# Writing the transposed keys and normalised rows contiguously, and reading them through permuted views

## The chip, the cores and the metric

The kernel runs on one core of a Trainium2 chip. The metric is the device time of one execution in microseconds (us). The engines are TensorE (PE, with its weight loads shown as PEld), VectorE (DVE), ScalarE (ACT), GpSimd (POOL) and SyncE (SP), which only issues DMAs here.

## What is computed

Three blocks follow one another on 8 x 576 rows of 512 numbers (all float32):

```python
# attention: 8 heads of 64, inside chunks of 64 rows
scores = scale * q_c @ k_c.T ;  attn = softmax(scores) ;  x = attn @ v_c
# first feed-forward block, w_ch1 512x2048, w_ch2 2048x512
xn = (x - mu) / sqrt(var + 1e-6) * g_ln
x1 = x + relu(xn @ w_ch1) @ w_ch2
# second block: a rank-32 mix along the 576 rows, then a feed-forward of the same size
u = x1 + (x1.T @ U @ V).T
out = u + relu(u @ w2_ch1) @ w2_ch2
```

## The kernel before, in words

The 4608 rows are 36 tiles of 128 rows. Attention and the first feed-forward work on twelve batches of three tiles. `g1` (L668) multiplies a batch with one of 16 slices of the first weight matrix: 12 matmuls of 384 columns into a PSUM tile `psh`, since each operand is split into a high and a low part and three of the four products are kept. ACT (L678) and DVE (L679) make the high and low parts of the result. `g2` (L682) multiplies these with the second matrix: 9 matmuls of 512 columns into `acc`. `finish` (L694) adds the sum to the residual. The loop at the end of `fused_kernel` writes the order of all this out by hand: one pair of `g1` and, two steps later, `g2` per step, with everything else hung on steps of that loop (`at`) or on thirds of a step (`at3`). An engine takes its instructions in exactly that order.

While one batch is multiplied, the attention and the normalisation of the tiles ahead are made beside it. Tiles 9 to 35 (27 tiles, the batches 3 to 11) go through these functions, in this order:

- `load_qk` (L329) brings q and k in by DMA, `st_A` (L377) turns both on DVE with a transpose that works on blocks of 32x32: L380 writes `qt`, L381 writes the key half of the tile `kt_pl`.
- `st_Bd` (L473) makes the scores with `quarters` (L368): 16 small float32 matmuls. `qt` is the stationary operand and `kt_pl` the moving one. The four quarters of the array are used side by side: two halves of the partitions (two heads) times two halves of the output (two chunks).
- `st_Cd`, `gather` and `st_T` (L504) turn the softmax weights, `st_D` multiplies them with v, `st_N` (L552) normalises: DVE at L563, then POOL at L564 times `g_ln`.
- `st_S` and `gather` send the normalised rows through HBM, and `st_E` calls `split` (L613): DVE turns them (L615) into a tile `wT`, ACT copies the high part into `act` (L617), POOL subtracts to get the low part (L618). `g1` of that batch reads both parts. `wT` and the normalised rows `xn` of the next tile share one buffer, so L563 of the next tile comes after L618.

Both transposes write their output through a view in which the 32 columns of a block lie four elements (16 bytes) apart: column number 4j + a, j counting 0 to 31 in the block and a the four blocks. So the reader finds the columns in natural order. Their inputs are read contiguously. The kernel's other block transposes are L504, L803 (reads 16 bytes apart, writes contiguously) and L965 (reads contiguously, writes 16 bytes apart). L661 is an ACT copy that reads 16 bytes apart.

In the same stretch the `pre_` functions (L183 to L266) prepare the weights of the second block on ACT and DVE and store them to HBM. After the last batch the second block runs, which the change does not touch.

Of the kernel before, what the change touches and what calls it, by code (L numbers as in the profile page):

```python
# [18 lines left out]
def fused_kernel(ctx, tc, q, k, v, g_ln, w1_a, w2_a, U, V, w1_b, w2_b, out):  # L19
    nc = tc.nc  # L20
# [20 lines left out]
    KT = DM // P  # L41
# [18 lines left out]
    def ps_tile(kind, shape):  # L60
        tags = banks[kind]
        turn[kind] += 1
        return psp.tile(shape, F32, tag=tags[turn[kind] % len(tags)], name="ps" + kind)

    def mm(o, l, r, start=True, stop=True, **kw):
        nc.tensor.matmul(o, lhsT=l, rhs=r, start=start, stop=stop, **kw)  # L66

    def f32(a):
        return a.bitcast(F32)
# [107 lines left out]
    pre = {}  # L177
# [149 lines left out]
    qk = {nm: qk6[:, 3 * m:3 * m + 3].rearrange("p t (a r i) -> p t a r i", a=4, r=4) for m, nm in enumerate(("q6", "k6"))}  # L327
# [15 lines left out]
    pl = {}  # L343
# [24 lines left out]
    def quarters(out, l, r):  # L368
        for pr in range(4):
            for h2 in range(2):  # L370
                pp = slice(64 * h2, 64 * h2 + 64)
                for c in range(2):
                    mm(out[h2][64 * c:64 * c + 64, ..., pr, :], l[pp, pr, 64 * c:64 * c + 64], r(pp, pr, c))
# [3 lines left out]
    def st_A(i):  # L377
        j, t = divmod(i, TPB)
        qt = t1.tile([P, 4, P], F32, tag="qt", name="qt")
        nc.vector.transpose(out=qt.rearrange("p r (j a) -> p a r j", a=4), in_=qk["q6"][:, t])  # L380
        nc.vector.transpose(out=pl["k"][:, 0].rearrange("p r (j a) -> p a r j", a=4), in_=qk["k6"][:, t])  # L381
        state["qt", i] = qt


# [88 lines left out]
    def st_Bd(i):  # L473
        qt = state.pop(("qt", i))
        sc = [ps_tile("m", [P, 2, 4, 32]) for _ in range(2)]
        quarters(sc, qt, lambda pp, pr, c: pl["k"][pp, 0, pr, 64 * c:64 * c + 64])
        m2 = st.tile([P, 2, 2, 2, 4], F32, tag="mx", name="mx")
        for h2 in range(2):
            nc.vector.tensor_reduce(out=m2[:, 0, h2].rearrange("p k r -> p (k r)"), in_=sc[h2].rearrange("p k r i -> p (k r) i"), axis=AX.X, op=ALU.max)
        nc.vector.tensor_tensor(out=m2[:, 1], in0=m2[:, 0, :, 0:1, :].to_broadcast([P, 2, 2, 4]), in1=m2[:, 0, :, 1:2, :].to_broadcast([P, 2, 2, 4]), op=ALU.max)  # L480
        e = t1.tile([P, DM], F32, tag="e", name="e")
        ev = e.rearrange("p (h g i) -> p h g i", h=2, i=32)
        for h2 in range(2):
            nc.vector.tensor_tensor(
                out=ev[:, h2], in0=sc[h2].rearrange("p k r i -> p (k r) i"),
                in1=m2[:, 1, h2].rearrange("p k (r o) -> p (k r) o", o=1).to_broadcast([P, 8, 32]), op=ALU.subtract,
            )
        nc.scalar.activation(out=e, in_=e, func=AF.Exp, scale=SCALE)
        state["e", i] = e
# [81 lines left out]
    def tiles_of(j):  # L571
        return [j * TPB + t for t in range(TPB)]

    def xt_tile(j, t):
        if t == 0:
            n = KT * P * len(tiles_of(j))
            o = (2 * n + 3 * BT) * (j % 2)
            xt[j] = tuple(act[:, o + m * n:o + (m + 1) * n].rearrange("p (k c) -> p k c", k=KT) for m in range(2))
        return (a[:, :, t * P:(t + 1) * P] for a in xt[j])
# [32 lines left out]

    def split(j, t, w, tag):  # L613
        x = t1.tile([P, KT, P], F32, tag=tag, name="wT")
        nc.vector.transpose(out=x.rearrange("p k (j a) -> p a k j", a=4), in_=w.rearrange("p a (k i) -> p a k i", k=KT))  # L615
        hi, lo = xt_tile(j, t)
        nc.scalar.copy(out=hi, in_=x)  # L617
        nc.gpsimd.tensor_tensor(out=lo, in0=x, in1=f32(hi), op=ALU.subtract)  # L618

# [3 lines left out]
    def st_E(i):  # L623
        split(i // TPB, i % TPB, state.pop(("w", i)), "xn")
# [497 lines left out]
    with tc.manual_schedule():  # L1122
# [23 lines left out]
        for n in range(2, NB):  # L1146
            g = NF * (n - 1)
            ends = []
            for t, i in enumerate(tiles_of(n)):
                if n == 2:  # L1150
                    s = (10, 15, 24)[t]
                    at(s - 6, load_qk_nat, i)
                    at(s, st_A_pe, i)
                    at(s + 1, st_B, i)
                    at(s + 2, st_C, i)
                    at(s + 3, st_D, i)
                    at(s + 3, load_v, i + 1)
                    if t == 0:
                        at(5, kv_tiles, i)
                        at(6, load_v, i)  # L1160
                    ends += [(pos[0, NF - 1] - 1 + t, st_N, i), (pos[0, NF - 1] + t, st_E_pe, i)]
                else:
                    s = g + {3: (2, 5, 8), 4: (-1, 2, 5), 5: (-2, 1, 5)}.get(n, (-3, 1, 5))[t]
                    at(s - (1 if n < 5 or t == 0 else 2), st_A, i)
                    at(s, st_Bd, i)
                    at(s + 1, st_Cd, i)
                    at(s + 2, gather, 2 * NT + i)
                    at(s + 3, st_T, i)
                    at(s + 5, st_D, i)
                    if i + 1 < NT:  # L1170
                        at(s + 5, load_v, i + 1)
                    s += 4 if n == 3 else 6
                    at(s + (n == 3), st_N, i)
                    at(s + 1, st_S, i)
                    at(s + 2, gather, i)
                    at(s + 3, st_E, i)
# [9 lines left out]
        for n in range(NB):  # L1186
# [6 lines left out]
            for t in range(TPB):  # L1193
                i = n * TPB + t
                r = i % 9
# [30 lines left out]
        free = [0, 0, 0]  # L1226
# [29 lines left out]
        x = PRE_G  # L1256
# [15 lines left out]
        for u in range(2 * NPR):  # L1272
# [2 lines left out]
            z = sums(u, y + 1)[1]  # L1275
            free[u % 2] = parts(u, z + g_pool, 1, 4)
            x += PRE_N[0]
        print("pre ends", free, file=__import__("sys").stderr)
        l2_first(at)

        load_qk_nat(0)
# [63 lines left out]
        for g in range(len(seq) + LAG):  # L1345
# [19 lines left out]
            j, f = seq[g - LAG] if LAG <= g < len(seq) + LAG else (0, 0)  # L1365
# [42 lines left out]
```

## Time and profile before

| | us |
|---|---|
| median of three runs (lowest to highest) | 1696.37 (1693.31 to 1698.58) |
| the profiled execution's own time | 1696.09 |
| its span, first to last instruction | 1694.2 |
| mean granted TensorE clock | 0.985 |

The span is what the trace shows; some 1.9 us of the time lie outside it. Matmul records overlap each other, so the busy time of PE says that something was in the array, not that it ran at its peak.

### The profile page before, as it was taken

How to read it: one execution, taken by the hardware profiler on the slowest of the kernel's cores; microseconds unless marked ns; L12 is line 12 of the kernel's file. 1: busy time of each engine (PE TensorE's matmuls, PEld its weight loads, DVE VectorE, ACT ScalarE, POOL GpSimd, SP SyncE). 2: the span in 40 equal slices, each digit the busy share in tenths (PEclk: the TensorE clock that was granted, in tenths of full speed). 3: DMA queues.
4: the chain of work that ended last, by engine and by line, in shares of the span. 5: the costliest groups of instructions: out<-in, count | busy, mean ns of one | idle time of the engine just before them, and what ended most of it. 6: DMA issues, size and time to landing. Idle time of an engine off the chain costs nothing.

```text
span 1694.2 us, 27810 instructions
## 1 busy us (share of the span) xinstructions
PE 1633.8 (96%) x9902; PEld 1423.1 (84%) x9902; DVE 1210.2 (71%) x2226; ACT 599.7 (35%) x1098; POOL 307.0 (18%) x291
## 2 busy tenths in 40 slices
PE   6899999999999999999999999999999999999997
PEld 5788878888788888888888899988887888888997
DVE  7887744577878787888874349739845983896496
ACT  5454411222232323323231134424443453334343
POOL 1000001111110211112021033043024303500421
PEclk8899999999999999999999999999999999999999
DMA  7353333546565556758553379888677887876885
GB/s 175 109 141 107 81 89 91 141 115 190 148 165 156 158 161 168 210 139 225 152 180 122 109 220 287 276 222 257 202 198 208 237 255 203 250 229 194 272 275 156
DMA packets 383948, 307.91 MB, mean 182 GB/s; under 512 B 192961, under 2 KB 280001, under 8 KB 383810
## 3 DMA queue, kind: packets, MB, share of 16 engines
q1 hardware_dynamic: 320802, 247.13, 52.3%
q10 hardware_dynamic: 63008, 59.00, 11.0%
q8 instruction: 80, 1.31, 0.3%
q14 instruction: 58, 0.48, 0.1%
HBM read 241.53 MB, written 64.49 MB: 181 GB/s over the span
## 4 chain that ended last, share of the span: by engine, by line
PE 62%; DMA 7%; DVE 4%; issue 1%; ACT 0%; SPq 0%; POOL 0%; ACTq 0%; DVEq 0%; POOLq 0%
PE ps L66 37%; PE acc L66 12%; PE psh L66 11%; DMA wr<-wd 3%; DMA zr<-zd 2%; PE psm L66 1%; DMA raw<-in_moe_w_ch 1%; DMA wd<-wsp 1%; PE zps L66 1%; PE pslow L66 1%; DMA wd<-wsq 0%; DVE zt L965 0%; DVE raw L228 0%; DMA out<-zt 0%; DVE act L679 0%
## 5 line engine op out<-in xcount | busy, mean ns | idle before, releaser
L66 PE MATMUL ps<-act,wr 128*128 128x512 f32 (+1 forms) x2100 | 445.7, 369 | 5.4 <-DMA wr<-wd 5.1
L66 PEld LDWEIGHTS ps<-act,wr 128*128 128x128 f32 x2100 | 382.8, 188 | 58.3 <-DMA wr<-wd 5.2
L66 PE MATMUL psh<-act,w0h 128*128 128x384 f32 x1536 | 398.9, 340 | 7.3 <-DVE act L679 2.7
L66 PE MATMUL acc<-w1h,act 128*128 128x512 f32 x1152 | 401.3, 402 | 1.5 <-DVE xbig L696 1.5
L66 PEld LDWEIGHTS psh<-act,w0h 128*128 128x128 f32 x1536 | 285.4, 191 | 27.1 <-DVE act L679 4.2
L66 PEld LDWEIGHTS acc<-w1h,act 128*128 128x128 f32 x1152 | 217.9, 189 | 58.8 <-issue 7.8
L66 PE MATMUL psh<-act,w0l 128*128 128x384 f32 x768 | 261.3, 340 | 0.9 <-DVE w0l L158 0.9
L679 DVE SCALAR_TENSOR_TENSOR act<-psh,act 128x384 fp32r<-128x384 f32 x192 | 106.7, 555 | 191.4 <-ACT act L678 190.9
L66 PE MATMUL acc<-w1l,act 128*128 128x512 f32 x576 | 228.8, 397 | 0.0
L678 ACT ACTIVATE act<-psh 128x384 fp32r<-128x384 f32 x192 | 93.8, 488 | 344.2 <-PE psh L66 279.5
L66 PEld LDWEIGHTS psh<-act,w0l 128*128 128x128 f32 x768 | 146.3, 190 | 1.2 <-DVE w0l L158 1.2
L66 PEld LDWEIGHTS acc<-w1l,act 128*128 128x128 f32 x576 | 109.0, 189 | 17.7
L618 POOL TENSOR_TENSOR act<-wT,act 128x512 fp32r<-128x512 f32 x27 | 34.9, 1293 | 307.2 <-ACT act L617 303.6
L544 POOL TENSOR_SCALAR rs<-mv 128x1 f32<-128x1 f32 x36 | 10.8, 301 | 402.7 <-DVE mv L542 394.4
L910 ACT ACTIVATE h<-h 128x512 f32<-128x512 f32 (+1 forms) x80 | 46.3, 588 | 102.8 <-DVE h L920 83.7
L916 DVE TENSOR_TENSOR h<-ps,h 128x512 f32<-128x512 f32 (+1 forms) x40 | 24.7, 632 | 69.7 <-PE ps L66 68.5
L197 ACT ACTIVATE raw<-raw 128x512 f32<-128x512 f32 x64 | 42.6, 674 | 55.0 <-DMA raw<-in_moe_w_ch 15.0
L654 POOL TENSOR_TENSOR zr<-zr 128x512 f32<-128x512 f32 x24 | 32.0, 1334 | 162.3 <-DMA zr<-zd 159.8
L903 POOL TENSOR_TENSOR h<-h,h 128x512 f32<-128x512 f32 (+1 forms) x40 | 51.8, 1316 | 36.2 <-DVE hr0l L890 15.6
L564 POOL TENSOR_TENSOR xn<-xn,gbc 128x512 f32<-128x512 f32 x27 | 38.6, 1428 | 50.2 <-DVE xn L563 50.2
L66 PE MATMUL ps<-hr0h,wr 128*128 128x512 f32 (+1 forms) x140 | 46.7, 373 | 0.3 <-issue 0.2
L66 PE MATMUL ps<-hr1h,wr 128*128 128x512 f32 (+1 forms) x140 | 46.0, 368 | 0.0
(218 smaller groups left out, 2558.3 us busy)
## 6 DMA issues: line engine op xcount, KB each, us to landing
wr<-wd SPq DMA_DIRECT2D x560, 256.0 KB
raw<-in_moe_w_ch SPq DMA_DIRECT2D x48, 512.0 KB
w<-sp ACTq DMA_DIRECT2D x54, 256.0 KB
wd<-wsp ACTq DMA_DIRECT2D x38, 256.0 KB
xw<-x1d SPq DMA_DIRECT2D x144, 64.0 KB
x1d<-xbig SPq DMA_DIRECT2D x34, 256.0 KB
v_pl<-in_v SPq DMA_DIRECT2D x132, 64.0 KB
out<-zt SPq DMA_DIRECT2D x132, 64.0 KB
```

Source lines behind the costliest of these rows:

```text
L66: nc.tensor.matmul(o, lhsT=l, rhs=r, start=start, stop=stop, **kw)
L197: nc.scalar.activation(out=w.bitcast(F32), in_=w.bitcast((F32, U32)[n]), func=AF.Copy, scale=2.0 ** (-112, -52)[n])
L544: nc.gpsimd.tensor_scalar(out=rs, in0=mv[:, 1:2], scalar1=1e-6, scalar2=None, op0=ALU.add)
L564: nc.gpsimd.tensor_tensor(out=xn, in0=xn, in1=gbc, op=ALU.mult)
L618: nc.gpsimd.tensor_tensor(out=lo, in0=x, in1=f32(hi), op=ALU.subtract)
L654: nc.gpsimd.tensor_tensor(out=zr[:, 0], in0=zr[:, 0], in1=zr[:, 1], op=ALU.add)
L678: nc.scalar.activation(out=hi, in_=ps, func=AF.Relu)
L679: nc.vector.scalar_tensor_tensor(out=lo, in0=ps, scalar=0.0, in1=f32(hi), op0=ALU.max, op1=ALU.subtract)
L903: nc.gpsimd.tensor_tensor(out=b11, in0=b12, in1=b11, op=ALU.subtract)
L910: relu = lambda a: nc.scalar.activation(out=a, in_=a, func=AF.Relu)
L916: vt(out=c12, in0=ps, in1=c12, op=ALU.add)
```

## The change

The two transposes write each block of 32 columns contiguously (column 32a + j in place of 4j + a). The readers get views that put the columns back in order: the score matmuls read `kt_pl` with a step of 32 elements inside groups of four, and so do ACT's copy and POOL's subtraction in `split`; what these two write is as before. A print at build time goes away. The transpose of q (L380) and that of the softmax weights (L504) stay.

```diff
 def st_A(i):
-    nc.vector.transpose(out=pl["k"][:, 0].rearrange("p r (j a) -> p a r j", a=4), in_=qk["k6"][:, t])
+    nc.vector.transpose(out=pl["k"][:, 0].rearrange("p r (a j) -> p a r j", a=4), in_=qk["k6"][:, t])
...
 def st_Bd(i):
-    quarters(sc, qt, lambda pp, pr, c: pl["k"][pp, 0, pr, 64 * c:64 * c + 64])
+    quarters(sc, qt, lambda pp, pr, c: pl["k"][pp, 0, pr].rearrange("p (a j) -> p j a", a=4)[:, 16 * c:16 * c + 16])
...
 def split(j, t, w, tag):
     x = t1.tile([P, KT, P], F32, tag=tag, name="wT")
-    nc.vector.transpose(out=x.rearrange("p k (j a) -> p a k j", a=4), in_=w.rearrange("p a (k i) -> p a k i", k=KT))
+    nc.vector.transpose(out=x.rearrange("p k (a j) -> p a k j", a=4), in_=w.rearrange("p a (k i) -> p a k i", k=KT))
     hi, lo = xt_tile(j, t)
+    x = x.rearrange("p k (a j) -> p k j a", a=4)
+    hi, lo = (a.rearrange("p k (j a) -> p k j a", a=4) for a in (hi, lo))
     nc.scalar.copy(out=hi, in_=x)
     nc.gpsimd.tensor_tensor(out=lo, in0=x, in1=f32(hi), op=ALU.subtract)
```

## Rows read from the trace of the kernel before

**Rows 1.** The page: busy time of PE and DVE, PE in 40 slices.
```profile
PE 1633.8 (96%) x9902; PEld 1423.1 (84%) x9902; DVE 1210.2 (71%) x2226; ACT 599.7 (35%) x1098; POOL 307.0 (18%) x291
...
PE   6899999999999999999999999999999999999997
```

**Rows 2.** Busy time by stage, 216 to 890: length, PE, PEld, DVE, ACT, POOL, clock.
```profile
216.00:890.00 674.00, 660.36 (x4798) 571.30 (x4797) 500.96 (x978) 188.48 (x358) 103.37 (x109) 1.00 0.56 155
```

**Rows 3.** Who PE waited for, 200 to 900: total, times, longest.
```profile
PE psm L66 <- DVE kt_pl L381: 10.7, 7, 3.6
...
PE psh L66 <- POOL act L618: 0.9, 1, 0.9
```

**Rows 4.** Groups of DVE: name, shapes, count, busy us, mean ns, idle before.
```profile
L615 DVE STREAM_TRANSPOSE wT<-w 128x512 f32<-128x512 f32 x27 | 29.6, 1098 | 8.7 <-DMA w<-sp 5.6 <-issue 1.9 <-DMA qk<-in_q 1.1
L380 DVE STREAM_TRANSPOSE qt<-qk 128x512 f32<-128x512 f32 x27 | 29.6, 1096 | 0.0
L381 DVE STREAM_TRANSPOSE kt_pl<-qk 128x512 f32<-128x512 f32 x27 | 29.1, 1078 | 0.0
...
L495 DVE TENSOR_REDUCE s<-e 128x16 f32<-128x512 f32 x27 | 17.7, 655 | 0.0
...
L106 DVE TENSOR_SCALAR qk<-qk 128x512 int32<-128x512 int32 x32 | 13.1, 409 | 0.0
...
L803 DVE STREAM_TRANSPOSE qk<-xw 128x512 f32<-128x512 f32 x10 | 11.0, 1096 | 0.0
...
L965 DVE STREAM_TRANSPOSE zt<-xbig 128x512 f32<-128x512 f32 x8 | 8.4, 1092 | 12.3 <-POOL xbig L949 12.3
```

**Rows 5.** Groups of ACT: a contiguous read and one 16 bytes apart.
```profile
L617 ACT CAST act<-wT 128x512 fp32r<-128x512 f32 x27 | 16.8, 621 | 61.6 <-DVE wT L615 61.6
...
L661 ACT CAST zs<-zr 128x512 fp32r<-128x512 f32 x8 | 8.8, 1106 | 13.9 <-POOL zr L654 13.9
```

**Rows 6.** Groups of POOL: the low part of the normalised rows.
```profile
L618 POOL TENSOR_TENSOR act<-wT,act 128x512 fp32r<-128x512 f32 x27 | 34.9, 1293 | 307.2 <-ACT act L617 303.6 <-DMA qk<-in_k 3.6
```

**Rows 7.** Timeline of PE at one score group: start, length, operation, records.
```profile
841.05 0.34 PE L66 MATMUL psh<-act,w0l 128*128 128x384 f32 x1
841.32 0.69 PE L66 MATMUL psm<-kt_pl,qt 64*64 64x64 f32 x32
841.94 0.50 PE L66 MATMUL acc<-w1h,act 128*128 128x512 f32 x1
```

**Rows 8.** The tile psm, 216 to 890: score matmuls, min/median/max ns.
```profile
L66 PE MATMUL psm<-kt_pl,qt x864: 218/218/312, 221.6 to 841.8; 64*64 64x64 f32 x173
```

**Rows 9.** Timeline of DVE before the longest wait for the keys.
```profile
424.62 0.56 DVE L679 SCALAR_TENSOR_TENSOR act<-psh,act 128x384 fp32r<-128x384 f32 x1 [0.85 <-ACT act L678]
...
429.12 1.06 DVE L380 STREAM_TRANSPOSE qt<-qk 128x512 f32<-128x512 f32 x1
430.04 1.04 DVE L381 STREAM_TRANSPOSE kt_pl<-qk 128x512 f32<-128x512 f32 x1
```

**Rows 10.** Timeline of DVE where two other such waits begin.
```profile
349.12 0.55 DVE L563 TENSOR_SCALAR xn<-xbig,mv,rs 128x512 f32<-128x512 f32 x1 [2.06 <-POOL act L618]
...
572.46 1.10 DVE L615 STREAM_TRANSPOSE wT<-w 128x512 f32<-128x512 f32 x1 [0.95 <-issue]
...
575.01 1.13 DVE L210 TENSOR_TENSOR raw<-raw,v_pl 128x512 f32<-128x512 f32 x1
```

**Rows 11.** Timeline of POOL: the subtractions at 574 and 666.
```profile
574.30 1.29 POOL L618 TENSOR_TENSOR act<-wT,act 128x512 fp32r<-128x512 f32 x1 [13.94 <-ACT act L617]
...
666.09 1.30 POOL L618 TENSOR_TENSOR act<-wT,act 128x512 fp32r<-128x512 f32 x1 [12.52 <-ACT act L617]
```

**Rows 12.** Timeline of PE: the first matmuls of batch 8.
```profile
668.02 0.51 PE L66 MATMUL psh<-act,w0h 128*128 128x384 f32 x2
```

More of the change, by code (lines that the diff above doesn't have):

```diff
@@ L1277, in fused_kernel @@
             x += PRE_N[0]
-        print("pre ends", free, file=__import__("sys").stderr)
         l2_first(at)
```

## The prediction

> **What bounds the kernel now.** I read the page first, then busy time by stage, then the waits. PE is busy for 96% of the span, and in every slice but the first two and the last at 90% or more [rows 1]. The changed operations run from 216 to 890 us. In these 674 us PE is busy for 660.4, DVE for 501.0, ACT for 188.5 and POOL for 103.4 [rows 2]. So PE sets the pace. Work taken off DVE can return at most what PE stood still, 674.0 - 660.4 = 13.6 us, while a matmul that takes longer is paid in full. The list of PE's waits says what of the 13.6 us the change can reach: 10.7 us in seven waits for the turned keys (L381), and 0.9 us in one wait for POOL's L618 [rows 3].
>
> The time is summed against the profiled execution's own 1696.09 us (span 1694.2 and 1.9 around it), which lies 0.3 us under the median, 1696.37.
>
> **The two transposes.** They take 1.078 us (keys) and 1.098 us (rows), 27 times each, as do all block transposes of 512 elements here; each of these has one side 16 bytes apart, the write in L380, L381, L615 and L965, the read in L803 [rows 4]. No row shows one with both sides contiguous. Ends: nothing is gained if turning 4-byte elements takes that long by itself; at best it runs like L106, 0.409 us. I take the nearest one-input pass over 512 floats, L495 with 0.655 us [rows 4], because on ACT the same 16-byte step accounts for a gap of that size: 1.106 us (L661) against 0.621 us (L617) [rows 5]. So L381 loses 0.42 us and L615 0.44 us. That is some 23 us less DVE work; what covers it is PE's own work, so only the waits count.
>
> **ACT's copy L617.** It now hops 128 bytes at every element. Ends: no cost if only the 16-byte step is slow, and L661's 1.106 us. I take the latter, the nearest row with scattered reads: +0.49 us [rows 5]. ACT has the room (188 of 674 us busy). Behind it in ACT's queue stands at most one L678, whose result `g2` needs two steps later; I cost that at nothing, and if the cover failed it would be 0.49 us at a place.
>
> **POOL's L618.** It takes 1.293 us [rows 6] and no row has POOL reading with a step. Ends: nothing, and a doubling, +1.29 us. I take ACT's surcharge per element, since it reads as many: +0.49 us. The end of L618 therefore moves by -0.44 + 0.49 + 0.49 = **+0.54 us**; between the ends, by -0.69 to +1.78 us.
>
> **What this does to the waits for the keys.** In each of the seven, L381 is the last thing to end. In the longest, DVE works without a pause from 424.62 to the end of L381 at 431.1, and nothing in that run gets shorter but L381 [rows 9]: 0.42 us back out of 3.6. Of the other six, five give 0.42 us too, and the smallest (0.25 us) vanishes: 6 x 0.42 + 0.25 = 2.8 us. Two of the seven runs begin at L618, though. At 349 us L563 starts only when L618 has let go of the shared buffer, after 2.06 us of idleness; at 575 us L210, right behind L615, is stretched to 1.13 us while L618 runs until 575.59 [rows 10, 11]. Both start 0.54 us later: +1.1 us. Sum for the keys: **-1.7 us** (ends: -5.8 and +3.6).
>
> **What it does at the start of a batch.** `g1` of the next batch needs the third tile's L618. Batch 3 waits for it already, so +0.54 us. Batch 8 has the smallest margin of the others: L618 ends at 667.39, the first matmul is at 668.02, 0.63 us [rows 11, 12]; the other seven, read the same way, have 1.26 to 2.36 us. These cover 0.54 us. Sum: **+0.5 us** (ends: -0.7 and, with the margins used up, +5.2).
>
> **The score matmuls.** This is the term that decides. They are the only changed work on PE itself: 27 groups of 16 float32 matmuls, two records each, 864 in all [rows 8]. One group holds PE from 841.32 to 841.94, 0.62 us [rows 7]. With four quarters of the array at work side by side, 32 records are eight rounds of 0.078 us, and a round streams 64 key columns. Before, four neighbours lay in 16 bytes; after, each column is 128 bytes from the last. No row shows PE reading with a step. Lower end: nothing, if PE fetches far enough ahead. A middle value: ACT pays (1106 - 621) / 512 = 0.947 ns more per scattered element [rows 5]; for 64 columns and eight rounds 0.485 us a group, 27 x 0.485 = 13.1 us. Upper end: the two halves of the output read the same 64 partitions, so the two key streams of a pair may have to take turns, 128 elements a round, 26.2 us. I take **+13.1 us**: in the rows a scattered step costs alike on every port that shows one, DVE's read, DVE's write and ACT's read [rows 4, 5], and float32 on PE leaves little slack, since a round of 0.078 us has 1.2 ns per column, less than the 1106 / 512 = 2.2 ns that ACT needs for one. The pause comes inside PE's own stream, with nothing to hide it; only what other engines owe PE gets easier by it.
>
> [...]
>
> **Sum.** 1696.09 - 1.7 + 0.5 + 13.1 = 1708.0 us, 0.7% slower.
>
> **The rivals.** *PE does not notice.* The reads are 64 columns long and could be fetched ahead while weights load; a 384-column record takes 0.34 us [rows 7], 0.9 ns a column, so PE's port delivers more than ACT's does. Against: the rates above. Then -1.7 + 0.5 remain: 1694.9 us, no change.
>
> *The two halves take turns.* For it: both streams of a pair lie in the same partitions, and today's score groups draw on four streams at once. Against: contiguous streams show no sign of it. 1696.09 - 1.2 + 26.2 = 1721.1 us. [...]
>
> *Faster: DVE catches up.* If PE reads the keys for nothing and 23 us less DVE work let DVE reach L381 ahead of PE, all seven waits and the one for L618 close: 1696.09 - 10.7 - 0.9 = 1684.5 us. It decides once L381 ends earlier by as much as the wait is long, up to 3.6 us. Against it: the run at 424 us starts from a wait for PE's own results and holds one shortened operation of 0.42 us.
>
> *The transposes do not get faster.* All show 1.08 to 1.10 us, whichever side has the step, so the time could be the transposer's. Then L618 ends 0.98 us later: two key waits +2.0, batch 3 +1.0, batch 8 +0.35; with the readers' price 1696.09 + 3.3 + 13.1 = 1712.5 us, without PE's part 1699.4.
>
> **How the numbers follow.** The forecast has 0.46, the unaffected PE 0.25, the two halves in turn 0.15, DVE catching up 0.06, transposes as slow as before 0.08 (0.06 with PE's price, 0.02 without). A measurement of this kernel tells about 0.3%, 5 us, from no change. Slower: 0.46 + 0.15 + 0.06, less 0.02 for a price on PE too small to be seen, 0.65. Same: 0.25 + 0.02 + 0.02 = 0.29. Faster: 0.06. The range starts at 1693, two microseconds under the case of an unaffected PE for the ends of the small terms, and goes to 1723, the same above the two halves in turn; it leaves out the faster case and the far ends.
>
> **What would show it.** Right: L381 and L615 near 0.66 us with L380 and L504 at 1.1; L617 near 1.1 and L618 near 1.8 us; the score group near 1.1 us from its first record to the next `acc` matmul; waits for L381 about 9 us in sum. Wrong: a score group still at 0.62 us (then no change), or at 1.6 us (then 1721), transposes still at 1.08 us, or no wait for L381 left.

## The result and the profile after

The changed kernel takes 1704.25 us, the median of seven runs (1701.03 to 1711.68); the kernel before, run beside it, 1696.37. The ratio is 1.0056 with a 95% interval of 1.0035 to 1.0076: slower, by some 9.5 us (5.9 to 12.9). The profiled execution took 1703.15 us, its span is 1701.3. From L617 on the line numbers are two higher: ACT's copy is now L619, POOL's subtraction L620.

The groups of the changed operations first (the columns as in [rows 4]), from the views of DVE, ACT and POOL:

```profile
L504 DVE STREAM_TRANSPOSE kt_pl<-w 128x512 f32<-128x512 f32 x27 | 29.7, 1101 | 10.6 <-DMA w<-sp 10.6
L380 DVE STREAM_TRANSPOSE qt<-qk 128x512 f32<-128x512 f32 x27 | 29.6, 1096 | 0.0
L615 DVE STREAM_TRANSPOSE wT<-w 128x512 f32<-128x512 f32 x27 | 19.1, 707 | 5.9 <-DMA w<-sp 3.1 <-issue 1.4 <-DMA qk<-in_q 1.3
L381 DVE STREAM_TRANSPOSE kt_pl<-qk 128x512 f32<-128x512 f32 x27 | 18.3, 679 | 0.0
...
L619 ACT CAST act<-wT 128x512 fp32r<-128x512 f32 x27 | 31.0, 1146 | 47.4 <-DVE wT L615 47.4
...
L620 POOL TENSOR_TENSOR act<-wT,act 128x512 fp32r<-128x512 f32 x27 | 43.1, 1597 | 309.1 <-ACT act L619 305.6 <-DMA qk<-in_k 3.6
```

DVE's two transposes fall from 1078 and 1098 ns to 679 and 707, while L380 and L504, not touched, stay at 1.1 us [rows 4]. The readers pay: ACT's copy goes from 621 to 1146 ns [rows 5], POOL's subtraction from 1293 to 1597 [rows 6].

What PE pays, in its timeline at one score group and in the list of the tile `psm` (min/median/max ns of 864 records):

```profile
849.43 0.34 PE L66 MATMUL psh<-act,w0l 128*128 128x384 f32 x1
849.70 1.11 PE L66 MATMUL psm<-kt_pl,qt 64*64 64x64 f32 x32
850.74 0.51 PE L66 MATMUL acc<-w1h,act 128*128 128x512 f32 x1
...
L66 PE MATMUL psm<-kt_pl,qt x864: 273/287/305, 222.0 to 850.5; 64*64 64x64 f32 x173
```

The group now holds PE from 849.70 to 850.74, 1.04 us where it was 0.62 [rows 7], and the record in the middle is 287 ns long where it was 218 [rows 8]. Over the 27 groups the mean rises from 0.630 to 1.044 us: 27 x 0.414 = 11.2 us.

Against that stand the waits (total, times, longest):

```profile
DVE xn L563 <- POOL act L620: 8.6, 3, 2.9
...
PE psm L66 <- DVE kt_pl L381: 8.1, 6, 2.6
```

PE waits 8.1 us for the keys in place of 10.7 [rows 3]; in the same list `xn`, which shares its buffer with `wT`, waits 8.6 us for POOL in place of 6.2. The last row that the prediction did not reckon with is the granted clock. Two stretches of the view of busy time by stage, and the whole stage (columns as in [rows 2]):

```profile
289.30:292.70 3.40, 3.40 (x10) 2.47 (x8) 2.28 (x6) 1.74 (x2) 1.14 (x1) 0.50 0.21 34
436.10:439.40 3.30, 3.30 (x10) 2.65 (x9) 3.20 (x9) 0.48 (x1) 0.00 (x0) 0.50 0.12 24
216.00:890.00 674.00, 664.49 (x4757) 574.12 (x4757) 485.40 (x964) 199.97 (x350) 108.06 (x107) 0.99 0.56 153
```

In both short stretches PE is never idle and has a clock of 0.50; both come soon after one of the long waits for the keys. In the first one a pair of 512-column matmuls takes 1.05 us (at 289.55), in the kernel before, at a clock of 1.00, 0.62 (at 288.21). By an estimate from the granted clock alone a stretch of 3.4 us at 0.50 does what takes 1.7 us at 1.00, so it costs up to 1.7 us. The changed kernel has two such stretches in this stage. The kernel before has one, after its longest wait:

```profile
431.60:435.00 3.40, 3.40 (x30) 2.70 (x23) 3.26 (x9) 0.00 (x0) 0.00 (x0) 0.51 0.39 106
```

The account for the stage: groups +11.2, waits for the keys -2.6, the wait at the start of batch 3 -0.7 (0.9 to 0.2), the wait for the residual (`xbig`) at its start -0.3 (1.57 to 1.25), two small waits that are gone (`g1` for L679 and for L617) -0.4, one more stretch at half clock +1.7, together +8.9 us. The first matmul of batch 11 came at 887.63 us before and comes here, in PE's timeline, at

```profile
896.43 0.51 PE L66 MATMUL psh<-act,w0h 128*128 128x384 f32 x2
```

which is 8.8 us later, as the account has it. These are the rows of one execution of each kernel. What follows, the last batch and the second block, takes 804.8 us to the end of the span (806.6 before), a scatter of that size being usual there: 801.7 to 808.7 in the experiments, none of which touches it.

### The profile page after: what moved, and what is told of

Read it like the earlier page. It is cut to its first block, busy times and chain, and to the rows that moved or that the text cites. A ratio compares the mean times of both kernels' runs of the same rounds, so it can differ in the third digit from the quotient of the medians.

```text
span 1701.3 us, 27810 instructions
## 1 busy us (share of the span) xinstructions
PE 1644.2 (97%) x9902; PEld 1432.1 (84%) x9902; DVE 1200.7 (71%) x2226; ACT 614.6 (36%) x1098; POOL 315.3 (19%) x291
## 2 busy tenths in 40 slices
DMA packets 383948, 307.91 MB, mean 181 GB/s; under 512 B 192961, under 2 KB 280001, under 8 KB 383810
## 4 chain that ended last, share of the span: by engine, by line
PE 64%; DMA 5%; DVE 4%; issue 1%; SPq 0%; POOL 0%; ACT 0%; DVEq 0%; POOLq 0%
PE ps L66 35%; PE acc L66 14%; PE psh L66 13%; DMA zr<-zd 2%; PE psm L66 2%; DMA xw<-x1d 1%; PE zps L66 1%; PE pslow L66 0%; DMA x1d<-xbig 0%; DVE zt L967 0%; DMA wr<-wd 0%; DMA raw<-in_moe_w_ch 0%; DMA wd<-wsq 0%; DVE xbig L827 0%; POOL zr L656 0%
## 5 line engine op out<-in xcount | busy, mean ns | idle before, releaser
L681 DVE SCALAR_TENSOR_TENSOR act<-psh,act 128x384 fp32r<-128x384 f32 x192 | 106.6, 555 | 213.8 <-ACT act L680 213.1
L620 POOL TENSOR_TENSOR act<-wT,act 128x512 fp32r<-128x512 f32 x27 | 43.1, 1597 | 309.1 <-ACT act L619 305.6
L544 POOL TENSOR_SCALAR rs<-mv 128x1 f32<-128x1 f32 x36 | 10.8, 301 | 404.3 <-DVE mv L542 396.0
L619 ACT CAST act<-wT 128x512 fp32r<-128x512 f32 x27 | 31.0, 1146 | 47.4 <-DVE wT L615 47.4
```

Of the source, the lines that this page charges most:

```text
L544: nc.gpsimd.tensor_scalar(out=rs, in0=mv[:, 1:2], scalar1=1e-6, scalar2=None, op0=ALU.add)
L681: nc.vector.scalar_tensor_tensor(out=lo, in0=ps, scalar=0.0, in1=f32(hi), op0=ALU.max, op1=ALU.subtract)
```

## The experiments

Each ratio is that of an experiment to the kernel before, run on the same chip.

### The two halves apart

`e1_rows_only` leaves the keys as they were:

```diff
-        nc.vector.transpose(out=x.rearrange("p k (j a) -> p a k j", a=4), ...)
+        nc.vector.transpose(out=x.rearrange("p k (a j) -> p a k j", a=4), ...)
+        x = x.rearrange("p k (a j) -> p k j a", a=4)
+        hi, lo = (a.rearrange("p k (j a) -> p k j a", a=4) for a in (hi, lo))
```

> Only the rows' half of the change: L615 writes contiguously, ACT's copy and POOL's subtraction read through the view; the keys are as before. Theory (the loss is PE's read of the keys): score groups stay at 0.62 us to the next matmul, L615 0.71, the ACT copy 1.15, the POOL subtraction 1.6 us; no change, 1695 to 1698 us (+0.0 to +0.1%). Rival (the loss comes from the rows, whose low part is ready later at batch starts and behind which DVE work queues): 5 us or more over before, 1701 or more.

Measured: 1.0020 (1.0002 to 1.0038), 3.4 us. L615 takes 706 ns, ACT's copy 1144, POOL's subtraction 1594; the score group stays at 0.64 us. The waits for the keys are 11.7 us in nine, more than before, and three stretches (286.6, 358.2 and 433.3 on) run at half clock. So the time falls between the two cases: the theory had at most 0.1%, the rival 5 us or more.

`e2_keys_only` is the other half:

```diff
-        nc.vector.transpose(out=pl["k"][:, 0].rearrange("p r (j a) -> p a r j", a=4), ...)
+        nc.vector.transpose(out=pl["k"][:, 0].rearrange("p r (a j) -> p a r j", a=4), ...)
...
-        quarters(sc, qt, lambda pp, pr, c: pl["k"][pp, 0, pr, 64 * c:64 * c + 64])
+        quarters(sc, qt, lambda pp, pr, c: pl["k"][pp, 0, pr].rearrange("p (a j) -> p j a", a=4)[:, 16 * c:16 * c + 16])
```

> Only the keys' half of the change: L381 writes contiguously and PE reads through the view; the rows are as before. Theory: score groups 1.04 us, 27 x 0.42 = 11.3 us dearer, the waits for L381 2.6 to 2.8 us less in sum: 1704 to 1706 us (+0.5%). Rival (the loss comes from the rows): no change or faster, 1693 to 1697 us.

Measured: 1.0040 (1.0022 to 1.0057), 6.8 us. L381 takes 678 ns, the group 1.044 us, the waits for the keys 5.7 us in five; they fall by 5.0 us, not by the 2.6 to 2.8 that were expected. Groups and waits make 11.2 - 5.0 = 6.2 us. The two halves add up to 0.60% where the whole change costs 0.56%: as far as intervals of 0.2% to either side tell, they don't act on each other.

### The key half taken apart

`e3_read_only` has the new view for PE and the old transpose:

```diff
-        quarters(sc, qt, lambda pp, pr, c: pl["k"][pp, 0, pr, 64 * c:64 * c + 64])
+        quarters(sc, qt, lambda pp, pr, c: pl["k"][pp, 0, pr].rearrange("p (a j) -> p j a", a=4)[:, 16 * c:16 * c + 16])
```

`e4_turn_only` has the new transpose and the old view:

```diff
-        nc.vector.transpose(out=pl["k"][:, 0].rearrange("p r (j a) -> p a r j", a=4), ...)
+        nc.vector.transpose(out=pl["k"][:, 0].rearrange("p r (a j) -> p a r j", a=4), ...)
```

> The kernel before with one edit: PE reads the keys through the view with a step of 32 elements, while L381 writes as before, so the scores have their keys in another order than v has. Theory: the price on PE alone, 27 x 0.42 = 11.3 us, and the waits for L381 stay near 10.7: 1706 to 1709 us (+0.65%). Rival (the step is not what costs, the tile written in runs of 32 is): score groups 0.62 us, 1695 to 1698 us.

> The kernel before with one edit: L381 writes contiguously, PE reads the tile contiguously, so the scores have their keys in another order than v has. Theory: what the cheaper transpose gives back without PE's price: L381 0.68 us, score groups 0.62 us, waits for L381 near 8.0 in place of 10.7: 1693 to 1695 us (-0.15%). Rival (DVE catches up with 11 us less work): waits for L381 under 3 us, 1688 us or less.

Measured: e3 1.0072 (1.0049 to 1.0096), e4 0.9988 (0.9970 to 1.0007). In e3 the group takes 1.044 us with a transpose of 1081 ns, so the pause is PE's reading and nothing else:

```profile
L381 DVE STREAM_TRANSPOSE kt_pl<-qk 128x512 f32<-128x512 f32 x27 | 29.2, 1081 | 0.0
...
L66 PE MATMUL psm<-kt_pl,qt x864: 273/287/304, 221.3 to 846.7; 64*64 64x64 f32 x173
```

(Its waits for the keys fall to 7.2 us where 10.7 were expected, perhaps because a slower PE leaves DVE time; the profiled execution was the shortest of nine, 1696.19 against a median of 1703.65, so its rows don't show all of the 0.72%.) In e4 the group takes 0.625 us, and of the waits this is left:

```profile
PE psm L66 <- DVE kt_pl L381: 5.6, 5, 1.7
```

The faster transpose alone saves 5.1 us of waits in the profile, where 2.8 were forecast for it (three executions below, with the same work on DVE, save 3.0 to 3.9), and the comparison can't tell the time from no change. The waits don't close: DVE does not catch up with PE.

### Which pattern costs PE its pause

Three single profiled runs, all with the new transpose of the keys, each with another view for PE (the added lines in the order `e5_runs16`, `e6_pairs`, `e7_step16`). They took 1691.97, 1695.32 and 1704.35 us, where nine runs of the kernel before have a median of 1690.35; one run each is too few to compare times, so the groups are read:

```diff
-  pl["k"][pp, 0, pr, 64 * c:64 * c + 64]
+  pl["k"][pp, 0, pr].rearrange("p (a j) -> p a j", a=4)[:, :, 16 * c:16 * c + 16]
+  pl["k"][pp, 0, pr].rearrange("p (a j w) -> p j a w", a=4, w=2)[:, 8 * c:8 * c + 8]
+  pl["k"][pp, 0, pr, 64 * c:64 * c + 64].rearrange("p (j a) -> p a j", a=4)
```

> The keys' half of the change, but PE reads each chunk in four runs of 16 adjacent columns, so the keys of the scores stand in another order than in v. If the price is for elements whose neighbour lies elsewhere, 4 breaks in 64 columns cost next to nothing: a score group takes 0.62 to 0.66 us to the next matmul. Rival (a view of two dimensions costs by itself): 1.04 us.

> As before it, but PE reads pairs of adjacent columns, 128 bytes from pair to pair (keys in another order than in v). If a port runs at full speed once it finds two elements in the same 16 bytes, a score group stays at 0.62 to 0.70 us. Rival (every break costs the same): half the breaks, half the price, 0.62 + 0.21 = 0.83 us.

> As before it, but PE reads with a step of 16 bytes (four elements) in runs of 16 columns (keys in another order than in v). If what counts is that no two elements that follow each other share 16 bytes, a score group takes 1.04 us as with the step of 128 bytes. Rival (the distance counts): between 0.62 and 0.95 us.

The records of the score matmuls in the list of the tile `psm`, runs of 16 columns, then pairs, then single columns 16 bytes apart:

```profile
L66 PE MATMUL psm<-kt_pl,qt x864: 218/218/313, 222.1 to 838.4; 64*64 64x64 f32 x173
```

```profile
L66 PE MATMUL psm<-kt_pl,qt x864: 213/216/288, 220.9 to 839.0; 64*64 64x64 f32 x173
```

```profile
L66 PE MATMUL psm<-kt_pl,qt x864: 273/292/308, 220.8 to 850.2; 64*64 64x64 f32 x173
```

The groups take 0.635, 0.628 and 1.071 us. Pairs of neighbours with 128 bytes from pair to pair take no longer than the contiguous read (0.628 us, 0.630 before). Single columns cost about as much with a step of 16 bytes as with one of 128. So it is neither the length of the hop nor the number of hops as such. In these runs the price came with single columns 16 or 128 bytes apart (1.071 and 1.044 us) and not with pairs of neighbours (0.628 us); e11_pairs_both below, with a step of 8 bytes, adds that two columns of 16 bytes that are not neighbours are enough (0.639 us). No row shows why that is so.

### Two ways out that keep the contiguous transpose

With PE reading runs of 16 columns the scores come out in another key order. `e8_runs16_v` loads v in that order too, so the softmax weights meet the right rows:

```diff
+                    vs = v[b, h2::2, s * CH:(s + 1) * CH, :].rearrange("h (j a) d -> a j h d", a=4)
+                    for a in range(4):
+                        p0 = 64 * h2 + 16 * a
+                        nc.sync.dma_start(out=pl["v"][p0:p0 + 16, 0, :, c, :], in_=vs[a])
```

> A version without PE's price: keys turned with contiguous writes, PE reads four runs of 16 columns a chunk, and v is loaded in the same order of keys, with four DMAs of 16 partitions in place of one of 64. Theory: L381 0.68 us, score groups 0.62 to 0.66 us, waits for L381 near 5.6 us: -0.1 to -0.3% against before. Rival (the 12 more DMA issues a tile, some 8 us of SP's time each tile, make k or v late): waits for v or for k's load on PE or DVE, no gain or slower.

Measured: 1.0445 (1.0421 to 1.0468), with groups of 0.659 us. Its waits, and its DMA issues of v:

```profile
ACT raw L197 <- DMA raw<-in_moe_w_ch: 49.8, 11, 9.4
...
PE psm L66 <- DVE kt_pl L387: 21.1, 8, 8.0
...
PE psm L66 <- DMA v_pl<-in_v: 8.8, 3, 6.2
```

```profile
v_pl<-in_v SPq DMA_DIRECT2D x432, 16.0 KB
v_pl<-in_v SPq DMA_DIRECT2D x24, 64.0 KB
```

432 loads of 16 partitions have taken the place of 108 of 64, and data that come by DMA are late: ACT waits 49.8 us for the weights (15.0 before), PE 8.8 us for v itself (0.2 before). The clock falls with it: its mean over the five runs is 0.970, against 0.988 in the nine of the kernel before, by an estimate from these means some 33 us of the 75 that were lost (0.030 x 1764 less 0.012 x 1688). The price came back in DMA, eight times the cost of the whole change. Which part of it is issuing on SP and which the smaller transfers was not separated.

`e9_psum_scatter` puts the hop on PE's output instead: the keys are read in four runs of 16 per matmul, and each result column is written to its place in PSUM, 16 bytes from the last:

```diff
+                kv_ = pl["k"][pp, 0, pr].rearrange("p (a c k j) -> p c a k j", a=4, c=2, k=2)
+                    o = sc[h2][64 * c:64 * c + 64, :, pr, :].rearrange("p k (j a) -> p a k j", a=4)
+                    mm(o, qt[pp, pr, 64 * c:64 * c + 64], kv_[:, c])
```

> A version that computes the reference: keys turned with contiguous writes (rows as before), PE reads each chunk in four runs of 16 adjacent columns, and puts the keys back in order where it writes: into PSUM, with a step of four elements. Theory (only the read from SBUF costs): score groups 0.62 to 0.66 us, waits for L381 near 5.6 us, -0.1 to -0.3% against before. Rival (a scattered write to PSUM costs as the scattered read does): score groups near 1.0 us, +0.4%.

The records of the score matmuls:

```profile
L66 PE MATMUL psm<-kt_pl,qt x864: 218/218/267, 221.0 to 837.3; 64*64 64x64 f32 x173
```

Measured: 0.9994 (0.9981 to 1.0007), groups of 0.625 us, L381 at 677 ns, waits for the keys 7.0 us. A step of 16 bytes, which costs 0.44 us a group on the read (e7_step16), costs nothing on the write to PSUM (0.625 us, as in e4_turn_only with a contiguous write). The time can't be told from no change. The waits of single executions also scatter: e4_turn_only, e5_runs16, e6_pairs and this kernel have the same work on DVE and groups of the same length, and show 5.6, 6.8, 7.7 and 7.0 us of waits for the keys.

### What the rows half pays

`e10_rows_read` has the new views for ACT and POOL and the old transpose: the readers' price without the transposer's gain.

```diff
+        x = x.rearrange("p k (a j) -> p k j a", a=4)
+        hi, lo = (a.rearrange("p k (j a) -> p k j a", a=4) for a in (hi, lo))
```

> The kernel before with one edit: ACT's copy and POOL's subtraction of the rows read through the view, while L615 writes as before, so the rows come out in another order. This has the readers' surcharge (0.52 and 0.30 us) without the cheaper transpose. Theory (the rows' half costs through the later end of POOL's subtraction, by 0.83 us here against 0.44 in the rows' half alone): +0.2 to +0.3%, waits of L563 and of PE for the subtraction longer than with the rows' half alone. Rival (the +0.2% of the rows' half is scatter between runs): within 0.1% of before, waits as before.

Measured: 1.0064 (1.0046 to 1.0082), more than was expected. L615 takes 1098 ns, the copy 1146, the subtraction 1592. The list of waits, and the stretches with a low clock (length, busy time of PE, PEld, DVE, ACT and POOL, then the clock):

```profile
PE psm L66 <- DVE kt_pl L381: 16.1, 9, 3.7
...
DVE xn L563 <- POOL act L620: 8.6, 3, 2.9
```

```profile
291.30:294.60 3.30, 2.92 (x9) 2.92 (x10) 0.00 (x0) 0.00 (x0) 0.33 (x1) 0.53 0.39 60
363.40:366.70 3.30, 3.30 (x10) 2.65 (x9) 2.75 (x7) 1.55 (x2) 0.80 (x1) 0.52 0.86 290
434.90:438.30 3.40, 2.14 (x35) 1.86 (x36) 3.33 (x7) 0.00 (x0) 0.00 (x0) 0.50 0.60 140
438.30:441.60 3.30, 3.30 (x10) 2.62 (x9) 3.23 (x8) 0.96 (x3) 0.00 (x0) 0.50 0.00 0
591.90:595.30 3.40, 3.40 (x9) 2.63 (x8) 3.30 (x9) 0.77 (x2) 0.00 (x0) 0.50 0.46 115
```

The waits for the keys rise by 5.4 us. Five stretches, 16.7 us in all, run at half clock, where the kernel before has one; at half the work of each that is up to 6.7 us more (less where PE stood still inside them). But this execution is the slowest of six, 1706.56 against a median of 1701.67, so its rows say too much of the usual one. Over all six the mean granted clock is 0.9852, over the 17 runs of the kernel before 0.9872: some 3.6 us, not 6.7. Waits and clock then make some 9 us of the 10.8 measured; the rest stays open. The step from here to e1_rows_only, the faster transpose, gives 4.4 us of waits back in the two profiles and by the mean clocks about 1 us, where 0.44% = 7.4 us were measured; some 2 us of that stay open too.

### A layout in which nobody pays

`e11_pairs_both` writes two neighbouring columns, then hops 32 bytes; the readers step 8 bytes and so take two elements of every 16 bytes, one after the other. It computes what the kernel before computes.

```diff
-  out=pl["k"][:, 0].rearrange("p r (j a) -> p a r j", a=4), in_=qk["k6"][:, t]
+  out=pl["k"][:, 0].rearrange("p r (j a w) -> p a r j w", a=4, w=2), in_=qk["k6"][:, t].rearrange("p a r (j w) -> p a r j w", w=2)
...
-  pl["k"][pp, 0, pr, 64 * c:64 * c + 64]
+  pl["k"][pp, 0, pr].rearrange("p (j a w) -> p j w a", a=4, w=2)[:, 8 * c:8 * c + 8]
```

`split` is changed in the same way.

> Both halves in a third layout: the two transposes write two neighbouring columns, then step 32 bytes on; PE, ACT and POOL step 8 bytes at every column, so each 16 bytes that they touch give them two following columns. The reference's function is computed in full. Theory (a port runs at full speed as long as every 16 bytes that it touches give it two following elements, whichever side writes or reads; only a lone element of 16 bytes is dear): L381 near 0.68 us and L615 near 0.70 as in the kernel after; the score group 0.62 to 0.66 us; ACT's copy 0.62 to 0.70; POOL's subtraction 1.29 to 1.35; the waits for L381 near 5.6 us as in e4; the time -0.1 to -0.4% of the kernel before, so a kernel that has both gains and neither price. Rival (any step other than 4 bytes is dear for an engine that reads it, or pairs are too short for the transposer's write): transposes still near 1.1 us, or a score group near 1.04 us and ACT's copy near 1.1: 0 to +0.6%.

Measured: 0.9976 (0.9959 to 0.9993), 1686.0 us, the median of ten runs, where the kernel before has 1690.46: some 4.1 us faster (1.2 to 6.9), and 0.8% under the changed kernel by the two ratios. Its groups, the records of the score matmuls, and the waits:

```profile
L615 DVE STREAM_TRANSPOSE wT<-w 128x512 f32<-128x512 f32 x27 | 19.2, 712 | 6.0 <-DMA w<-sp 3.2 <-issue 1.6 <-DMA qk<-in_q 1.1
L381 DVE STREAM_TRANSPOSE kt_pl<-qk 128x512 f32<-128x512 f32 x27 | 18.5, 686 | 0.0
...
L619 ACT CAST act<-wT 128x512 fp32r<-128x512 f32 x27 | 18.1, 669 | 48.3 <-DVE wT L615 48.3
...
L620 POOL TENSOR_TENSOR act<-wT,act 128x512 fp32r<-128x512 f32 x27 | 35.4, 1309 | 296.4 <-ACT act L619 296.4
```

```profile
L66 PE MATMUL psm<-kt_pl,qt x864: 215/219/270, 220.9 to 835.3; 64*64 64x64 f32 x173
```

```profile
PE psm L66 <- DVE kt_pl L381: 5.5, 5, 2.4
```

Both transposes keep their gain (686 and 712 ns), the copy pays 48 ns, the subtraction 16, the score group takes 0.639 us, and the waits for the keys fall by 5.2 us. With one stretch at half clock, as before, that is the gain that the change was in a position to make.

## Why the prediction was right

**The verdict and its cause.** 1708.0 us was forecast with a range of 1693 to 1723, and 1704.25 measured. The cause named was the price of the scattered read on PE; e3_read_only has that alone and is slower, e4_turn_only has the rest of the key half and isn't. The size was taken from ACT's surcharge, 0.947 ns per element or 0.485 us a group; the runs show 0.414 us, 0.81 ns per column. So the term of 13.1 us was 1.9 us too large. That the time came so near is in part luck: +11.9 us were forecast, the rows of the two profiles add up to +8.9, and among the errors are two of opposite sign, waits put 2.1 us too dear and 1.7 us of half clock that were not in the sum.

**The transposes.** 0.42 and 0.44 us less were forecast from the nearest one-input pass, 0.40 and 0.39 measured. That both sides contiguous would be faster was not on any row before; the runs show it, and pairs are as good (686 and 712 ns).

**The copy and the subtraction.** ACT's +0.49 us is +0.525 in the trace. POOL's +0.49 is +0.30: ACT's surcharge per element does not hold for POOL. The end of the subtraction moves by -0.39 + 0.525 + 0.30 = +0.43 us, forecast +0.54. The place where this reaches DVE stands in its timeline, L615 of the kernel before, then the two rows of the changed one, the counterpart of [rows 10]:

```profile
345.96 1.10 DVE L615 STREAM_TRANSPOSE wT<-w 128x512 f32<-128x512 f32 x1
...
349.42 0.70 DVE L615 STREAM_TRANSPOSE wT<-w 128x512 f32<-128x512 f32 x1
352.96 0.55 DVE L563 TENSOR_SCALAR xn<-xbig,mv,rs 128x512 f32<-128x512 f32 x1 [2.84 <-POOL act L620]
```

From the start of L615 to L563 it is 3.54 us; it was 3.16 (345.96 to 349.12).

**The waits.** Forecast for keys and batch starts together -1.2 us, measured -3.3: the keys -2.6 (forecast -1.7), batch 3 -0.7 (forecast +0.5). For the keys the difference is no more than the scatter between single executions shown above; the far end of -5.8 us comes out near -5.5 from the seven waits, and nothing rests on it. The longest wait gave back 1.0 us where 0.42 was forecast:

```profile
431.23 0.84 PE L66 MATMUL psm<-kt_pl,qt 64*64 64x64 f32 x32 [3.64 <-DVE kt_pl L381]
...
434.39 1.11 PE L66 MATMUL psm<-kt_pl,qt 64*64 64x64 f32 x32 [2.64 <-DVE kt_pl L381]
```

DVE's part is near the forecast: its run from L679 (L681 after) to the end of L381 lasts 6.13 us in place of 6.46. The other 0.7 us come from PE, which reaches the group 3.6 us after that run begins, in place of 3.0; why it does was not looked into. The other batch starts were covered as the prediction said: the smallest margin left between L620 and the first `g1` is 0.93 us. For batch 3 the step failed: the later subtraction was put down in full, but one of the stretches at half clock lies right ahead of that `g1` (289.3 to 292.7), so PE comes to it later and waits 0.2 us. That it is the clock and not the slower score groups is what three runs say: e1_rows_only, with such a stretch there and fast groups, waits 0.5 us; e3_read_only, with such a stretch (287.8 on) and slow groups, doesn't wait; e2_keys_only, with slow groups and no such stretch, waits the old 0.9.

**The term that was missing.** The rows half was forecast at +1.1 + 0.5 = 1.6 us; e1_rows_only shows 3.4 (0.3 to 6.4). Its waits for the keys rise by 1.0 us, about as forecast, though that is within their scatter. The larger part is the clock: the profiled execution has two more stretches at half clock, up to 2 x 1.7 = 3.4 us, and over all runs the mean granted clock is 0.9856 in the 12 of e1_rows_only and 0.9870 in the 32 of the kernel before beside them, 0.0014 x 1693 = some 2.4 us. The prediction has no term for it. A row hinted at one: in the kernel before the longest wait is followed by such a stretch, so a longer wait can cost more than it lasts. It gives no size, though, since the wait of 2.35 us at 581 in the same trace is followed by none. e10_rows_read, with longer waits still, has a mean clock of 0.9852.

**The rivals.** *PE does not notice* fell with e3_read_only. *The two halves take turns* fell by its size: it wanted 0.97 us more a group, 0.41 were measured. *DVE catches up* fell with e11_pairs_both, where both transposes are fast, PE reads for nothing and 5.5 us of waits remain (5.6 in e4_turn_only, with the keys' transpose alone). *The transposes do not get faster* fell with 679 and 707 ns. In every pattern that was run, a reader paid for single elements 16 or 128 bytes apart and little or nothing for two out of every 16 bytes: PE took 1.071 us a group with steps of 16 bytes and 1.044 with steps of 128, but 0.628 with pairs and 0.639 with steps of 8; ACT's copy 1146 ns with steps of 128 bytes and 669 with steps of 8; POOL's subtraction 1597 and 1309.

## What to carry to other kernels

Here the scattered access, moved from the writer to its readers, took its price along (0.414 us a score group on PE, 0.525 us a copy on ACT, 0.30 us a subtraction on POOL), so ask first which engine sets the pace: 21 us less work on DVE were worth about 5 us of waits here, and 0.41 us more per score group on PE were paid in full. Before choosing a side, try a layout like that of e11_pairs_both (for float32, write pairs and read with a step of 8 bytes), which kept the transposes at 686 and 712 ns and the readers at 0.639 us, 669 and 1309 ns, or let PE scatter its results into PSUM, which in e9_psum_scatter had no price (0.625 us a group) but brought no gain clear of the scatter either.

## What was not expected

- A step of 8 bytes was free, or nearly, for PE, ACT and POOL (0.639 us a group, 669 and 1309 ns, where contiguous reads took 0.630, 621 and 1293), although no two following elements are neighbours.
- PE wrote float32 results with a step of 16 bytes into PSUM without loss (0.625 us a group, as with the contiguous write of e4_turn_only).
- For single columns PE's price hardly depended on the hop: 1.071 us a group at 16 bytes, 1.044 at 128.
- A wait of PE for the keys was often followed by some 3.4 us at half clock, which by the estimate above add up to 1.7 us to it: those of 1.98 and 2.64 us in the changed kernel, the one of 1.53 us at 429 in e2_keys_only (clock 0.98 from 400 to 500 us), the four of 2.7 to 3.7 us in e10_rows_read. It does not always happen: the wait of 2.35 us in the kernel before and the one of 2.18 us in e3_read_only were followed by none.
- Loading v in 432 pieces of 16 partitions in place of 108 of 64 made the kernel 4.45% slower, with 307.95 MB moved by DMA in place of 307.91.
